# An attention block and a two-of-eight expert layer on one core: from 28 pair buckets to one list of slots per expert with the results added up in memory

## The chip, the core and the metric

The kernel runs on one core of one Trainium2 chip, in one launch. The metric is device time in microseconds: the median over the runs of the kernel, lower is better. Times inside a profile are microseconds from the start of the profiled span.

## What is computed

First a chunked attention over 4 batches, 8 heads, 768 tokens and 64 values per head: each chunk of 32 queries sees 8 memory keys of its batch and head and a window of 56 keys (16 to the left, its own 32, 8 to the right). Its output, with heads side by side, is a matrix x of 3072 tokens by 512. Then a noisy top-2 layer of 8 experts:

```python
noisy_logits = x @ w_gate + np.log1p(np.exp(x @ w_noise)) * noise
top2 = np.argpartition(-noisy_logits, 2, axis=1)[:, :2]
# top2_w: softmax over the two logits
for e in range(8):
    for k in range(2):
        mask = top2[:, k] == e
        h = np.maximum(x[mask] @ w1[e], 0.0)
        out[mask] += top2_w[mask, k, None] * (h @ w2[e])
```

`w1` is 512 by 1024 and `w2` is 1024 by 512 for each expert, all float32 in memory; the kernel computes in bfloat16. Every token goes to exactly two experts, so 6144 rows pass through an expert.

## The kernel before

**Attention.** The 32 heads of the 4 batches are worked on as 16 pairs (`NPAIR`), loaded in 8 groups of 2 pairs by `load_qk` (L109) and `load_v` (L118). These loads change float32 to bfloat16 on the way and are issued on GpSimd's queue (POOL). There are three buffers of each kind, so a load of group g waits until group g-3 is used up. A pair goes through TensorE transposes of q and k (L216, copied by ScalarE at L218), scores (L230 to L243), a maximum and a difference on VectorE (L251), an exponential on ScalarE, transposes of the probabilities, the product with v (`ps_o`, L279 and L282) and a division on VectorE into `xrow` (L294). The main loop over `i` (from L462 on) writes the order of every engine out by hand.

**Routing.** After 4 pairs a batch is complete. `route(b)` finds the two experts of each token, its gates and its rank within its bucket, and SyncE writes the batch's rows (`x_rows<-xrow`, 1056 bytes a token: 512 bfloat16 values and 8 gates) to memory.

**Experts.** A bucket holds the tokens that share the same pair of experts: 28 buckets with 128 slots each, and one spill tile of 32. Since a bucket belongs to two experts, its 128 rows are gathered once (`gather`, L580), transposed once into `xTb` (L589 copied at L590), and used by both. Expert e computes 7 buckets and the spill: `first` (L644) multiplies 928 columns by `w1`, relu alternates between ScalarE (L630) and VectorE (L632), `second` (L652) multiplies each of 7 tiles by `w2`. Of the two experts of a bucket the earlier leaves its scaled result in one of 20 accumulators on chip (ScalarE, L656); the later adds to it (VectorE, L659) and the row goes out by one scatter (L660). So `out` is written once and never read. Weights are loaded two experts ahead on POOL's queue by `load_w1` (L439) and `load_w2` (L444), three buffers each.

A loop for more than 32 spilled tokens stands at the end of the kernel; with the data used here it is not entered.

Of the kernel before, what the change touches and what calls it, by code (L numbers as in the profile page):

```python
# [14 lines left out]
F32R = mybir.dt.float32r  # L15
# [5 lines left out]
I32 = mybir.dt.int32  # L21
# [3 lines left out]
def kernel(  # L25
# [14 lines left out]
    nc = tc.nc  # L40
# [12 lines left out]
    HP = H // 2  # L53
    WIN = left_ctx + chunk + right_ctx
    CTX = WIN + n_mem
    SJ = S // 128
    assert D == 64 and CTX == 64 and 4 * chunk == 128 and S == 128 * SJ
    NPAIR = B * HP
    GP = 2
    NG = NPAIR // GP  # L60
    CAP = 128
    NB = E * (E - 1) // 2
    NB4 = E * (E // 2)
    SPILL = 32
    XC = Dm // 2
    ROW = XC + E
    FAR = 8 * N
    NEG = -1e30

    def bucket(a, b):  # L70
        d = b - a
        return (d - 1) * E + a if d <= E // 2 else (E - d - 1) * E + b

    xd = nc.dram_tensor("x_rows", [N, ROW], I32, kind="Internal").ap()
    xd_part = dram_disjoint_views(xd, B + 1)
    out_part = dram_disjoint_views(out, NB + 1)
# [4 lines left out]
    w1p = ctx.enter_context(tc.tile_pool(name="w1p", bufs=3))  # L81
    w2p = ctx.enter_context(tc.tile_pool(name="w2p", bufs=3))

    def body():
        actx = ExitStack()
        ap_ = actx.enter_context(tc.tile_pool(name="ap", bufs=2))
        psS = actx.enter_context(tc.psum_pool(name="psS", bufs=1))
        psO = actx.enter_context(tc.psum_pool(name="psO", bufs=1))
        psT = actx.enter_context(tc.psum_pool(name="psT", bufs=3))
        psL = actx.enter_context(tc.psum_pool(name="psL", bufs=1))  # L90

        nc.scalar.preload_act_table_set("natural_log_exp_and_others")


        groups = {}

        vbufs = [ap_.tile([128, GP, ncnk, 2, D], BF16, name=f"vg{i}", bufs=1) for i in range(3)]

        def new_group(g):
            qg = ap_.tile([128, 2 * GP, SJ * D], BF16, name="qg", bufs=3)  # L100
            kg = ap_.tile([128, 2 * GP, SJ * D], BF16, name="kg", bufs=3)
            groups[g] = (qg, kg, vbufs[g % 3])

        def load_qk(g, i=None):
            qg, kg, _ = groups[g]
            b, h0 = divmod(2 * GP * g, H)
            hs = slice(0, 2 * GP) if i is None else slice(2 * i, 2 * i + 2)
            for dst, src in ((qg, q), (kg, k)):
                nc.gpsimd.dma_start(out=dst[:, hs, :], in_=src[b, h0:h0 + 2 * GP][hs].rearrange("h (p j) d -> p h (j d)", p=128))  # L109
# [705 lines left out]
```

## Time and profile before

| | |
|---|---|
| median of 2 runs | 396.87 us (396.57 and 397.17) |
| span of the profiled execution | 393.1 us; 3.8 us of the median lie around it |
| PE (TensorE) busy | 304.5 us, 77% of the span |
| DVE (VectorE) busy | 169.9 us, 43% |
| ACT (ScalarE) busy | 119.8 us, 30% |
| POOL (GpSimd) busy | 124.5 us, 32% |
| moved by DMA | 42.93 MB in 83324 packets |

The profile gives busy times per engine, the same in stretches of the span ("windows", with the TensorE clock that was granted, the share of time in which the DMA engines worked, and the rate), the chain of work that ended last, groups of equal instructions with their mean duration, waits by what ended them, and a timeline. A share of DMA above 1 in a window means that packets of several transfers stood in the engines at once. PE, PEld, DVE, ACT and POOL are TensorE's products, its weight loads, VectorE, ScalarE and GpSimd; SP is SyncE, which only starts transfers here.

### The profile page before, as it was taken

The numbers are of one execution on the slowest core, as the hardware profiler recorded it, in microseconds if no ns is written. First come the engines' busy times: TensorE is split into PE (matmuls) and PEld (weight loads), VectorE is DVE, ScalarE is ACT, GpSimd is POOL, SyncE is SP. The second block draws the span as 40 slices with busy tenths as digits, with TensorE's granted clock in tenths as the row PEclk, the third lists the DMA queues.
The fourth block names the chain that finished last, engine by engine and source line by source line (L and its number), as shares of the span: only waits on it lengthen the run. The fifth ranks groups of instructions, "written<-read, shape, count | busy, mean of one in ns | idle before, by whom it ended". The sixth has DMA issues, their size and how long they took to land.

```text
span 393.1 us, 9217 instructions
## 1 busy us (share of the span) xinstructions
PE 304.5 (77%) x4042; PEld 188.6 (48%) x4060; DVE 169.9 (43%) x350; ACT 119.8 (30%) x235; POOL 124.5 (32%) x143
## 2 busy tenths in 40 slices
PE   0448688676846433888998998999998999999990
PEld 0436566454634322654465474454454454544540
DVE  7426345787757761342142242241433242443340
ACT  1436354565532200222333232233221312302200
POOL 7766234265000026352100420520605123032061
PEclk9999555898885655699999999999999999999997
DMA  9999999999970412849700291291492921811021
GB/s 92 100 164 156 158 152 94 167 150 141 211 154 3 143 46 80 151 82 216 141 0 2 45 221 30 64 209 34 97 213 88 191 56 71 132 67 70 3 115 59
DMA packets 83324, 42.93 MB, mean 109 GB/s; under 512 B 57255, under 2 KB 76711, under 8 KB 83280
## 3 DMA queue, kind: packets, MB, share of 16 engines
q0 software_dynamic: 74928, 38.85, 70.6%
q1 hardware_dynamic: 8064, 3.38, 3.4%
q8 instruction: 34, 0.56, 0.6%
q10 hardware_dynamic: 288, 0.07, 0.1%
q14 instruction: 10, 0.08, 0.1%
HBM read 61.32 MB, written 10.65 MB: 183 GB/s over the span
## 4 chain that ended last, share of the span: by engine, by line
PE 60%; DVE 15%; issue 10%; DMA 7%; ACT 3%; POOL 3%; POOLq 0%; DVEq 0%; ACTq 0%
PE ps_h L644 24%; PE ps_y L652 21%; DMA x_rows<-xrow 4%; PE p_t L216 3%; DMA kg<-in_k_dram 2%; PE ps_o L279 2%; PE ps_o L282 2%; DVE xrow L294 2%; PE p_t L589 2%; DVE vg L130 2%; DVE xTb L590 2%; POOL out_dram L660 2%; DVE mx L251 1%; ACT qT L218 1%; PE p_x L303 1%
## 5 line engine op out<-in xcount | busy, mean ns | idle before, releaser
L644 PE MATMUL ps_h<-xTb,w1t 128*128 128x512 bf16 (+3 forms) x608 | 107.8, 328 | 1.1 <-DVE xTb L590 1.0
L652 PE MATMUL ps_y<-w2t,ht 128*128 128x512 bf16 x430 | 98.9, 379 | 1.0 <-issue 0.2
L644 PEld LDWEIGHTS <-w1t 128*128 128x128 bf16 x864 | 64.7, 98 | 45.0 <-issue 1.1
L632 DVE TENSOR_SCALAR ht<-ps_h 128x416 bf16<-128x416 f32 (+2 forms) x68 | 41.7, 613 | 81.0 <-PE ps_h L644 81.0
L660 POOL DMA_INDIRECT out_dram<-acc,sidx x28 | 28.0, 998 | 144.9 <-DVE acc L659 142.4
L652 PEld LDWEIGHTS <-ht 128*128 128x128 bf16 x448 | 42.3, 98 | 48.9
L630 ACT ACTIVATE ht<-ps_h 128x416 bf16<-128x416 f32 (+2 forms) x68 | 36.3, 535 | 87.2 <-PE ps_h L644 83.1
L580 POOL DMA_INDIRECT xl<-x_rows,gidx x28 | 29.1, 1038 | 71.4 <-DVE ov1b L523 48.4
L644 PE MATMUL ps_h<-xTs,w1t 128*128 128x32 bf16 x256 | 45.4, 177 | 0.2 <-DVE xTs L605 0.2
L118 POOL DMA_DIRECT2D vg<-in_v_dram x34 | 32.9, 974 | 35.4 <-PE ps_o L282 29.8
L656 ACT ACTIVATE acc<-ps_y,meta 128x512 f32<-128x512 f32 x28 | 19.2, 687 | 76.5 <-PE ps_y L652 47.7
L659 DVE SCALAR_TENSOR_TENSOR acc<-ps_y,meta,acc 128x512 f32<-128x512 f32 x28 | 21.0, 751 | 38.6 <-PE ps_y L652 38.6
L590 DVE COPY xTb<-p_t 128x512 bf16<-128x512 bf16 x28 | 11.8, 423 | 27.1 <-PE p_t L589 26.9
L218 ACT CAST qT<-p_t 128x384 bf16<-128x384 f32 x32 | 16.9, 586 | 20.2 <-PE p_t L216 20.2
L216 PE MATMUL p_t<-identb,kg 128*64 128x128 bf16 x192 | 14.1, 275 | 10.5 <-ACT qT L218 7.7
L251 DVE TENSOR_REDUCE mx<-ps_s 128x12 f32<-128x768 f32 x16 | 15.2, 950 | 12.1 <-PE ps_s L243 12.1
L305 ACT COPY xt<-p_x 128x768 bf16<-128x768 bf16 x16 | 12.8, 799 | 22.5 <-PE p_x L303 22.5
L216 PE MATMUL p_t<-identb,qg 128*64 128x128 bf16 x192 | 11.5, 265 | 9.5 <-DMA qg<-in_q_dram 5.1
L279 PE MATMUL ps_o<-memv,PT 128*128 128x132 bf16 x96 | 11.2, 273 | 9.4 <-DVE PT L270 9.4
L589 PE MATMUL p_t<-identb,xl 128*128 128x128 bf16 x112 | 11.2, 224 | 8.9 <-DVE xTb L590 8.9
L218 ACT CAST kT<-p_t 128x384 bf16<-128x384 f32 x32 | 17.0, 597 | 2.0 <-PE p_t L216 1.7
L294 DVE TENSOR_TENSOR xrow<-ps_o,rec 128x768 bf16<-128x768 f32 x16 | 15.3, 958 | 5.3 <-DMA x_rows<-xrow 4.8
(128 smaller groups left out, 295.5 us busy)
## 6 DMA issues: line engine op xcount, KB each, us to landing
w1t<-in_moe_w_dram POOLq DMA_DIRECT2D x8, 1024.0 KB
w2t<-in_moe_w_dram POOLq DMA_DIRECT2D x8, 1024.0 KB
vg<-in_v_dram POOLq DMA_DIRECT2D x30, 168.0 KB
x_rows<-xrow SPq DMA_DIRECT2D x3, 792.0 KB, 6.3
qg<-in_q_dram POOLq DMA_DIRECT2D x6, 384.0 KB
kg<-in_k_dram POOLq DMA_DIRECT2D x6, 384.0 KB
qg<-in_q_dram POOLq DMA_DIRECT2D x4, 192.0 KB
kg<-in_k_dram POOLq DMA_DIRECT2D x4, 192.0 KB
```

The lines of the kernel that those rows point to most:

```text
L118: nc.gpsimd.dma_start(out=vg[p0 + j:p0 + j + nj, x, c:c + n, hh, :], in_=bass.AP(v.tensor, v.offset + (hd * S + c * chunk + j - left_ctx) ...
L216: nc.tensor.matmul(out=p_t[64 * hh:64 * hh + 64, j, :], lhsT=src[:, 2 * i + hh, (SH * x + j) * D:(SH * x + j + 1) * D], rhs=identb, start= ...
L218: nc.scalar.copy(dst[:, :, SH * x:SH * (x + 1)], p_t.rearrange("d j p -> d p j"))
L294: nc.vector.tensor_tensor(out=xr, in0=po.rearrange("p x (u h) c -> p x u h c", h=2)[:, :, :, :, :D], in1=rec.rearrange("p x (u h o) -> p x ...
L580: nc.gpsimd.indirect_dma_start(out=xl, out_offset=None, in_=xd, in_offset=bass.IndirectOffsetOnAxis(ap=gidx[:, p:p + 1], axis=0), bounds_c ...
L590: nc.vector.tensor_copy(xTv[:, :, p, :], p_t)
L630: nc.scalar.activation(out=dst, in_=src, func=Act.Relu)
L632: nc.vector.tensor_scalar(out=dst, in0=src, scalar1=0.0, scalar2=None, op0=Alu.max)
L644: nc.tensor.matmul(out=ps_h[:, o:o + w], lhsT=w1t[:, kp, f * 128:(f + 1) * 128], rhs=rhs(kp), start=(kp == 0 and i == 0), stop=(kp == KP - ...
L652: nc.tensor.matmul(out=ps_y, lhsT=ht[:, f, j * CAP:(j + 1) * CAP], rhs=w2t[:, f, :], start=(f == 0), stop=(f == FB - 1))
L659: nc.vector.scalar_tensor_tensor(out=a, in0=ps_y, scalar=gate, in1=a, op0=Alu.mult, op1=Alu.add)
L660: nc.gpsimd.indirect_dma_start(out=out_part[p], out_offset=bass.IndirectOffsetOnAxis(ap=sidx[:, p:p + 1], axis=0), in_=a, in_offset=None, ...
```

## The change

Everything in the kernel is written anew, around four decisions.

**A list scheduler sets the order.** Each step is an operation with candidate engines, an assumed duration, dependences, buffers and a priority. `Planner.run` simulates them and returns the operations in order of their simulated start; this is the order in which they are issued. Its costs are assumptions in the code: 1.05 for an indirect transfer plus 0.25 to 0.35 and 1.8 to 1.9 until it has landed, 3.0 and 3.4 for the two weight loads, 1.4 for a load of q or k, 3.1 for half a load of v.

**One list of slots per expert.** `x_lists` in memory has 3136 rows of 1060 bytes (values, gates, token number) for each expert. A batch writes each token's row to both of its lists: 12 indirect scatters per batch on POOL (L641), 48 in all, in place of one direct write by SP. The slots of an expert then lie side by side, so SP loads them with direct transfers (L684, L687) and the 28 gathers of rows are gone. Each expert computes 832 slots: a part of 512 and a tail of 320, whose last 64 rows are spread over two half rows each. All counts are below 832 for this data (715 to 808), so the loop at the end is not entered.

**Two experts are closed early.** Experts 0 and 1 take 512 slots from the first three batches alone ("sealed"), so their first parts need nothing from the last batch. Parts run in this order: sealed 0, sealed 1, experts 2 to 7 (512 and 320), tails of 0 and 1.

**Results are added up in memory.** `out` is filled with zeros by four SP transfers of 1.5 MB, and unused slots of the lists are blanked by one of 1.1 MB. Each tile of results is gathered from `out` (L751), added on VectorE (L776) and scattered back (L787); only sealed 0 scatters without gathering. That makes 52 gathers and 56 scatters in place of 29 scatters. A gather waits for all scatters of the experts before it, since two experts can share a token. In the expert stage relus are on ScalarE and additions on VectorE; 8 PSUM banks of one kind serve transposes, first and second products.

The attention keeps its steps. q and k are loaded as 96 partitions of 8 tokens, v in halves of 2 heads; the weights of experts 0 and 1 use buffers of their own and are loaded during attention.

```diff
-    CAP = 128
-    NB = E * (E - 1) // 2
-    SPILL = 32
+    CAPE = 3136
+    SEAL = 512
+    NSEAL = 2
+    CAP = 832
...
+    xs = nc.dram_tensor("x_lists", [E * CAPE, ROW], I32, kind="Internal").ap()
+    xs_part = dram_disjoint_views(xs, 2 * NP)
...
+    def run(self):
...
+                for eng, dur in o.engs:
+                    est = max(free.get(eng, 0.0), at)
+                    for d in o.deps:
+                        est = max(est, d.end if d.eng == eng and not d.dma else d.done)
+                    if best is None or est + dur < best[0] + best[2]:
+                        best = (est, eng, dur)
+                cand.setdefault(best[1], []).append((best[0], best[2], o))
...
+            for eng, cs in cand.items():
+                m = min(c[0] for c in cs)
+                c = min((c for c in cs if c[0] <= m + 0.25), key=lambda c: (c[2].prio, c[0]))
+                if pick is None or c[0] < pick[0]:
+                    pick = (c[0], c[1], c[2], eng)
...
+                xfer, lat = o.dma
+                dma_free = max(o.end + 0.6, dma_free) + xfer
+                o.done = dma_free + lat
...
+        return sorted(order, key=lambda o: o.start)
...
+        def qk_load(o, bb, src, b=b, h0=h0):
+            G_.dma_start(out=bb.t, in_=src[b, h0:h0 + 4].rearrange("h (p j) d -> p h (j d)", p=QP))
...
+            piece(int(first), 2 * ncnk - first - last)
+
+        zd = z_v[g] if g < 3 else []
+        lv = [op(("POOL", 1.3 if 0 < g < NG - 1 else 2.0), lambda o, hh=hh, f=v_load: f(o, hh), deps=zd, alloc=[bv] if hh == 0 else [], use=[] if hh == 0 else [bv],
+                 prio=pr + 6 + hh if g else 2 + hh, dma=(3.1, 1.6), tag="attn") for hh in range(2)]
...
+    c_fill = op(("SP", 0.1), lambda o: nc.sync.dma_start(
+        out=xs.rearrange("(e c) r -> c e r", c=CAPE)[CAP - 128:CAP], in_=blank.rearrange("p (o r) -> p o r", o=1).to_broadcast([128, E, ROW])),
+        deps=[z_bl, groups[1][4]], prio=20, dma=(3.0, 1.8))
...
+    c_zero = [op(("SP", 0.1), lambda o, i=i: nc.sync.dma_start(
+        out=out[i * S:(i + 1) * S].rearrange("(t p) d -> p t d", p=128), in_=zero.rearrange("p (o d) -> p o d", o=1).to_broadcast([128, BT, Dm])),
+        deps=[z_zero] + groups[NG - 1][5], prio=10.0 * NPAIR + i, dma=(2.8, 1.8)) for i in range(B)]
...
+                    G_.indirect_dma_start(
+                        out=xs_part[(b * BT + t) * 2 + kk], out_offset=bass.IndirectOffsetOnAxis(ap=R["idx"][:, t, kk:kk + 1], axis=0),
+                        in_=xr.t[:, t, :], in_offset=None, bounds_check=E * CAPE - 1, oob_is_err=True)
...
+                scat[b].append(op(("POOL", 1.05), scatter, deps=[r7, c_fill], use=[xr], prio=pr + 1 + 0.1 * t, dma=(0.25, 1.8)))
...
+    parts = []
+    for e in range(NSEAL):
+        parts.append(dict(e=e, s0=0, sealed=True, grp=e))
+    for x, e in enumerate(list(range(NSEAL, E)) + list(range(NSEAL))):
+        if e >= NSEAL:
+            parts.append(dict(e=e, s0=0, sealed=False, grp=NSEAL + x))
+        parts.append(dict(e=e, s0=SEAL, sealed=False, grp=NSEAL + x))
+    W = {}
...
+    def w_load(e, prio):
+        b1, b2 = buf("w1"), buf("w2")
+        o1 = op(("POOL", 0.85), lambda o: G_.dma_start(out=b1.t, in_=moe_w1[e].rearrange("(kp p) f -> p kp f", p=128)), alloc=[b1], prio=prio, dma=(3.0, 1.8))
+        o2 = op(("POOL", 0.95), lambda o: G_.dma_start(out=b2.t, in_=moe_w2[e].rearrange("(fb p) d -> p fb d", p=128)), alloc=[b2], prio=prio + 1, dma=(3.4, 1.8))
+        W[e] = (b1, b2, o1, o2)
+
+    for e in range(E):
+        w_load(e, 10.0 * 13.5 + e if e < NSEAL else 10.0 * NPAIR + 100 * e)
...
+            nc.sync.dma_start(out=bxl.t[:, :nf, :], in_=xs[r0:r0 + nf * 128].rearrange("(j p) r -> p j r", p=128))
+            if not full:
+                for hh in range(2):
+                    nc.sync.dma_start(out=bxl.t[64 * hh:64 * hh + 64, 2, :], in_=xs[r0 + 256:r0 + 320])
...
+        prev = [s for gnum in range(grp) for s in scatters.get(gnum, [])] + c_zero
...
+            def gather(o, b, R=R, t=t, w=w, oview=oview, bound=bound):
+                G_.indirect_dma_start(
+                    out=b.t[:, :w], out_offset=None, in_=oview(out), in_offset=bass.IndirectOffsetOnAxis(ap=R["ids"][:, t:t + 1], axis=0),
+                    bounds_check=bound, oob_is_err=False)
+
+            ga = None
+            if not plain:
+                ga = op(("POOL", 1.05), lambda o, f=gather, ba=ba: f(o, ba), deps=[oi] + prev, alloc=[ba], prio=pr + 6 + 0.1 * t, dma=(0.35, 1.9))
+            gy = buf("G", quota)
...
+                if plain:
+                    A.activation(out=ba.t[:, :w], in_=gy.t[:, :w], func=Act.Copy, scale=gate)
+                else:
+                    V.scalar_tensor_tensor(out=ba.t[:, :w], in0=gy.t[:, :w], scalar=gate, in1=ba.t[:, :w], op0=Alu.mult, op1=Alu.add)
+            yo = op(("ACT", 0.7) if plain else ("DVE", 0.25 + w / 960), yev, deps=[so, ga, lx] + (z_acc if plain else []), alloc=[ba] if plain else [], use=[gy, bxl] + ([] if plain else [ba]), prio=pr + 20 + t)
+            if plain and grp:
+                bb = buf("acc")
+                ga = op(("POOL", 1.05), lambda o, f=gather, bb=bb: f(o, bb), deps=[oi] + prev, alloc=[bb], prio=pr + 40 + 0.1 * t, dma=(0.35, 1.9))
+                yo = op(("DVE", 0.6), lambda o, ba=ba, bb=bb: V.tensor_tensor(out=ba.t, in0=ba.t, in1=bb.t, op=Alu.add), deps=[yo, ga], use=[ba, bb], prio=pr + 41)
...
+            def oscat(o, ba=ba, R=R, t=t, w=w, nv=nv, oview=oview, bound=bound):
+                G_.indirect_dma_start(
+                    out=oview(out_part[nv]), out_offset=bass.IndirectOffsetOnAxis(ap=R["ids"][:, t:t + 1], axis=0),
+                    in_=ba.t[:, :w], in_offset=None, bounds_check=bound, oob_is_err=False)
+
+            scatters.setdefault(grp, []).append(op(("POOL", 1.05), oscat, deps=[yo, oi] + c_zero, use=[ba], prio=pr + 20 + t, dma=(0.35, 1.8)))
```

Three places of the new order. The first is POOL's queue early in the attention, where the loads of group 3 begin (`qn` and `kn` are q and k, `vg` is v, `w1t` and `w2t` are the weights of experts 0 and 1):

```order
L376 DMA kn_103<-in_k_dram 96x4x512 [waits DMASW4_49,PE_49]
L659 DMA w1t_67<-in_moe_w_dram 128x4x1024 [waits DMASW5_49]
L376 DMA qn_101<-in_q_dram 96x4x512 [waits DMASW6_49,PE_49]
L660 DMA w2t_69<-in_moe_w_dram 128x8x512 [waits DMASW7_49]
L376 DMA kn_104<-in_k_dram 96x4x512 [waits DMASW0_49,PE_49]
L659 DMA w1t_68<-in_moe_w_dram 128x4x1024 [waits DMASW1_49]
L660 DMA w2t_70<-in_moe_w_dram 128x8x512 [waits DMASW2_49]
L387 DMA vg_105<-in_v_dram 56x48x64 [waits DMASW3_49,PE_49]
L387 DMA vg_105<-in_v_dram 56x48x64 [waits DMASW4_49]
```

All four weight loads of 1 MB now stand ahead of the two v loads of group 3; before, three weight loads stood behind the last v load of the whole attention:

```order
L118 DMA vg_89<-in_v_dram 48x64 [waits DMASW6_49]
L118 DMA vg_89<-in_v_dram 56x23x64 [waits DMASW7_49]
L439 DMA w1t<-in_moe_w_dram 128x4x1024 [waits DMASW0_49]
L444 DMA w2t<-in_moe_w_dram 128x8x512 [waits DMASW1_49]
L439 DMA w1t<-in_moe_w_dram 128x4x1024 [waits DMASW2_49]
L580 DMA xl<-x_rows,gidx 128x264 [waits DMAHW1_49,DMAHW2_49,DMAHW0_49,DMAHW3_49,DMASW3_49,DMAHW7_49,DVE_49,Activation_49]
```

The second place is POOL at the end of attention, between the scatters of the third batch (`xrow_87`) and of the last (`xrow_85`), with the weights of experts 2 and 3 between them (`w1l`, `w2l`):

```order
L641 DMA x_lists<-xrow_87,idx 25088x265 [waits DMASW5_49]
L659 DMA w1l_2976<-in_moe_w_dram 128x4x1024 [waits DMASW6_49,PE_49]
L660 DMA w2l_2978<-in_moe_w_dram 128x8x512 [waits DMASW7_49,PE_49]
L659 DMA w1l_2977<-in_moe_w_dram 128x4x1024 [waits DMASW0_49]
L660 DMA w2l_2979<-in_moe_w_dram 128x8x512 [waits DMASW1_49]
L641 DMA x_lists<-xrow_85,idx 25088x265 [waits DMAHW4_49,DMAHW5_49,DMASW2_49,DVE_49]
L641 DMA x_lists<-xrow_85,idx 25088x265 [waits DMASW3_49]
L641 DMA x_lists<-xrow_85,idx 25088x265 [waits DMASW4_49]
L641 DMA x_lists<-xrow_85,idx 25088x265 [waits DMASW5_49]
L641 DMA x_lists<-xrow_85,idx 25088x265 [waits DMASW6_49]
```

Rows further on wait for the transfers eight places ahead, so the fifth to eighth scatter of the last batch wait for the four weight loads to have landed. On PE, the first tile of expert 2 (`xll0`, loaded from the lists after all scatters) stands ahead of the products of sealed 1 (`w1t1`):

```order
L717 LDWEIGHTS xl1_72
L717 MATMUL ps_l3_3003<-identb_130,xl1_72 128x128
L717 LDWEIGHTS xll0_2980 [waits DMAHW6_49]
L717 MATMUL ps_l4_3004<-identb_130,xll0_2980 128x128 [waits DVE_49]
L717 LDWEIGHTS xll0_2980
L717 MATMUL ps_l4_3004<-identb_130,xll0_2980 128x128
L731 LDWEIGHTS w1t1_68 [waits DVE_49]
L731 MATMUL ps_l5_3005<-xT1_74,w1t1_68 128x512 [waits Activation_49]
```

What was behind the whole of sealed 1 in the list of parts is thus ahead of its first product in TensorE's order.

The third place is POOL during expert 3, from its last first-part gather to the first gather of expert 4 (L751 gathers from `out`, L787 scatters to it):

```order
L787 DMA out_0_dram<-acc4_81,ids_3281 3072x512 [waits DMASW4_49,DMASW5_49,DMASW3_49,DMASW6_49,DMASW2_49,DVE_49]
L787 DMA out_0_dram<-acc7_84,ids_3281 3072x512 [waits DMASW0_49,DVE_49]
L787 DMA out_0_dram<-accl1_2989,ids_3281 3072x512 [waits DVE_49]
L751 DMA accl0_2988<-out_0_dram,ids_3410 128x512 [waits DMASW7_49,DMASW1_49,DMASW0_49]
L787 DMA out_0_dram<-accl3_2991,ids_3281 3072x512 [waits DMASW2_49,DVE_49]
L751 DMA accl2_2990<-out_0_dram,ids_3410 128x256 [waits DMASW3_49]
L659 DMA w1l1_2977<-in_moe_w1_dram 128x4x1024 [waits PE_49]
L787 DMA out_0_dram<-acc6_83,ids_3410 3072x512 [waits DMASW4_49,DVE_49]
L787 DMA out_0_dram<-accl0_2988,ids_3410 3072x512 [waits DVE_49]
L660 DMA w2l1_2979<-in_moe_w2_dram 128x8x512 [waits PE_49]
L787 DMA out_0_dram<-accl2_2990,ids_3410 6144x256 [waits DVE_49]
L751 DMA accl4_2992<-out_0_dram,ids_3578 128x512 [waits DMASW7_49,DMASW6_49,DMASW1_49]
```

Before, the same place held scatters that no gather waited for, and gathers of rows that were there since attention:

```order
L439 DMA w1t<-in_moe_w_dram 128x4x1024 [waits DMASW7_49,PE_49]
L660 DMA out_dram<-acc_3309,sidx 3072x512 [waits DMASW0_49,DVE_49]
L660 DMA out_dram<-acc_3304,sidx 3072x512 [waits DMASW1_49,DVE_49]
L660 DMA out_dram<-acc_3298,sidx 3072x512 [waits DMASW2_49,DVE_49]
L444 DMA w2t<-in_moe_w_dram 128x8x512 [waits DMASW3_49,PE_49]
L580 DMA xl<-x_rows,gidx 128x264 [waits DMASW4_49,Activation_49]
L580 DMA xl<-x_rows,gidx 128x264 [waits DMASW5_49,Activation_49]
L439 DMA w1t<-in_moe_w_dram 128x4x1024 [waits DMASW6_49,PE_49]
```

Now gathers and scatters alternate, each waiting for the other to have landed, with the weight loads of expert 5 among them.

1175 lines of the change are left out of this document (561 added, 614 removed).

## The prediction

> **What bounds the kernel now.** I read the windows first, cut where the work changes, then the chain that ended last. In the windows the columns are length, busy time of PE, PEld, DVE, ACT and POOL, granted TensorE clock, DMA share and GB/s.
>
> ```profile
> 43.00:63.00 20.00, 15.73 (x394) 12.65 (x394) 10.22 (x15) 9.24 (x18) 7.49 (x8) 0.50 1.92 153
> 115.00:131.00 16.00, 9.28 (x203) 7.64 (x203) 12.62 (x29) 3.53 (x5) 0.00 (x0) 0.57 0.14 42
> 195.00:383.00 188.00, 183.57 (x1400) 97.68 (x1412) 64.86 (x106) 47.68 (x93) 46.16 (x47) 1.00 0.42 90
> 383.00:393.10 10.10, 0.11 (x1) 0.00 (x0) 0.75 (x1) 0.00 (x0) 1.41 (x2) 0.77 0.15 58
> ```
>
> There are two kernels in one. From 195 on PE works 183.57 of 188 us at full clock, seven experts of 26.9 us each, with DMA at 0.42: bound by PE. Before that no engine is full, and the transfers are another matter:
>
> ```profile
> DMA  9999999999970412849700291291492921811021
> POOL vg L118 <- PE ps_o L282: 29.8, 9, 5.3
> L294 DVE TENSOR_TENSOR xrow<-ps_o,rec x16: 957/958/958, 32.3 to 131.7; 128x768 bf16<-128x768 f32 x16
> 65.00:70.00 5.00, 0.96 (x1) 0.74 0.81 52
> 15.98 9.09 DMA kg<-in_k_dram
> 100.86 14.07 DMA x_rows<-xrow
> 128.25 3.34 DMA x_rows<-xrow
> ```
>
> The first row is the DMA engines' share in 40 slices of 9.8 us: at least 0.9 for the first 108 us. Yet POOL had room: its v loads waited 29.8 us for buffers that PE still used, so loads were ahead of compute. The third row is the division that ends each head pair, 16 times from 32.3 to 131.7; the seventh pair's falls in the window of the fourth row (that operation alone, one execution), at about 67. The last three are pieces of the chain: start, length, what. A 384 KB load took 9.09 us because others stood ahead in its queue, and 14.07 and 3.34 us were spent on the x rows, whose write shared the engines with weights. So this stage has no slack in transfers worth speaking of, and 17.4 us of pure waiting.
>
> **The change, part by part.** *What it saves.* PE's rows in an expert:
>
> ```profile
> 244.75 6.91 PE ps_y L652 x32
> 251.66 12.90 PE ps_h L644 x96
> L589 PE MATMUL p_t<-identb,xl 128*128 128x128 bf16 x112 | 11.2, 224 | 8.9 <-DVE xTb L590 8.9
> ```
>
> The first products take 12.90 us for 928 columns, so 11.6 for 832; four tiles of second products take 6.91, so the 6.5 tiles of an expert 11.2, with the half-row tail about 11.5; seven tiles of transposes are 28 of 224 ns in groups of four that overlap, some 1.6. PE needs 24.7 us an expert, in place of 26.9. If PE stayed the bound, eight experts would need 198 us. The 17.4 us on x rows fall away too.
>
> *Transfers ahead of group 3's v.* POOL's order puts four weight loads ahead of these v loads, and SP's four zero fills wait only for a memset, so they run at once. Prices, from windows in which one kind ran (weights, weights, q and k, v, output rows):
>
> ```profile
> 282.50:288.50 6.00, 6.00 (x48) 3.30 (x46) 2.33 (x4) 2.23 (x4) 2.45 (x3) 1.00 1.08 159
> 289.50:294.50 5.00, 4.95 (x37) 2.66 (x36) 1.93 (x3) 1.07 (x4) 0.05 (x1) 1.00 1.09 210
> 30.00:31.00 1.00, 1.00 (x13) 0.81 (x11) 0.00 (x0) 0.88 (x2) 0.36 (x1) 1.00 1.32 201
> 53.50:55.50 2.00, 1.19 (x22) 1.17 (x24) 0.76 (x2) 0.21 (x2) 1.42 (x2) 0.50 2.14 128
> 384.00:387.50 3.50, 0.00 (x0) 0.00 (x0) 0.00 (x0) 0.00 (x0) 0.98 (x1) 1.00 0.41 156
> ```
>
> 1 MB of weights at 159 to 210 GB/s is 5.0 to 6.6 us; I take 6.25 (four: 25). 384 KB of q or k at 201 is 2.0 (twelve: 24). Half a group of v is 344 KB, at 128 GB/s 2.6 (eight: 21). For rows of 2 KB written, 156 GB/s at a share of 0.41 is 380 at a full one: the 7.4 MB of zeros and blanks take 19 us, or 47 if they only get the 156; 19, because the row is the same kind of packet. With some 4 us until the first load the sum is 4 + 24 + 21 + 25 + 19 = 93 us for group 3's v. The seventh pair needs it at about 67 now, so it is 26 to 28 us late. The lower bound is no delay at all, if the fills and weights fit into gaps; against it speaks the row of nines. The nine later pairs took 131.7 - 67 - 17.4 = 47 us, so attention ends at about 142, and with the last ranking at 145.
>
> *The last batch's lists.* Prices of indirect transfers, in timelines of POOL and ACT:
>
> ```profile
> 143.89 1.16 POOL L580 DMA_INDIRECT xl<-x_rows,gidx  x1 [48.42 <-DVE ov1b L523]
> 145.35 1.04 POOL L580 DMA_INDIRECT xl<-x_rows,gidx  x1 [0.30 <-issue]
> 146.70 1.01 POOL L580 DMA_INDIRECT xl<-x_rows,gidx  x1 [0.30 <-issue]
> 147.04 0.20 ACT L591 COPY meta<-xl 128x8 f32<-128x8 f32 x1 [7.82 <-DMA xl<-x_rows,gidx]
> 384.17 0.98 POOL L660 DMA_INDIRECT out_dram<-acc,sidx  x1 [0.74 <-DVEq L738]
> 280.70 0.99 POOL L444 DMA_DIRECT2D w2t<-in_moe_w_dram  x1
> 284.41 0.85 POOL L439 DMA_DIRECT2D w1t<-in_moe_w_dram  x1
> ```
>
> One is issued every 1.3 us, and 3.1 us after its issue (143.89 to 147.04) another engine uses what came. I count 2.6 us to landing and 0.3 to the next issue. A scatter's is bounded by 384.17 and the 3.3 us to the end of its window, so the same value serves. The third batch's 12 scatters, queued behind the second's, run until 152.5; four weight loads are issued until 156 and move data until 179 or so; the fifth to eighth scatter of the last batch wait for these to land, and with four more behind them the last one lands at 188. The load of expert 2's first tile adds 3, an estimate from the same rows: X = 191. Since PE has that tile's transposes ahead of sealed 1's first product, sealed 1 cannot fill this gap; sealed 0 alone is done inside it. Now the first product of the expert stage starts at about 156 (chain: 157.69), so the early part costs 30 to 35 us.
>
> *An expert, by POOL's order.* Time from its first gather: five gathers 4 x 1.3 + 2.6 = 7.8; three scatters at 8.1, 9.4 and 10.7, landed at 13.3; a gather at 13.6, landed 16.2; a scatter at 16.5, landed 19.1; a gather at 19.4, landed 22.0; w1 issued at 20.7; two scatters at 22.3 and 23.6; w2 at 24.9; the last scatter at 25.9, behind 12.5 us of weights in the same queue, so landed at about 35.9. The next expert's first gather follows at 36.2. The additions in between cost little beside it:
>
> ```profile
> L659 DVE SCALAR_TENSOR_TENSOR acc<-ps_y,meta,acc 128x512 f32<-128x512 f32 x28 | 21.0, 751 | 38.6 <-PE ps_y L652 38.6
> ```
>
> 36.2 is more than PE's 24.7, so the chain of landings is the new bound. Its bounds: 24.7, if it all hides behind PE, and 36.2 + 0.75 for each of six alternations, 41. Expert 2 has its weights and needs 33.
>
> *The sum.* From X to expert 2's first gather 25 us (sealed 1's products, scatters and gathers); expert 2 33; experts 3, 4 and 5 36.2 each; so expert 6 begins at X + 166.6. It loads no weights: 28.5. Expert 7, seven gathers and then seven scatters, 9.1 + 2.6 + 0.3 + 9.1 + 2 = 22.5 or so. The first tail 12.3; the second 6.5 and its scatters, with the 8.9 us from the last scatter's issue (384.17) to the end of the span (393.1): 15.4. Together 78.7, so the span is 191 + 166.6 + 78.7 = 436, and with the 3.8 around it **440 us**; the profiled execution was 396.9 by the same addition, the same as the median of the runs.
>
> *The clock.* At 43 to 63 PE was busy for 79% and got a clock of 0.50; at 115 to 131, busy for 58%, 0.57. In the new expert stage it is busy for 68%, so it may not get a full clock there. At half, an expert takes PE 49.4 us in place of 24.7, and PE is the bound again. [...]
>
> **The rivals.**
>
> *A, PE stays the bound (faster).* Evict and gather overlap through eight PSUM banks and fourteen accumulators, early transfers fit into gaps. Then attention ends at 131.7 - 14 = 118, lists follow after four weight issues, twelve scatters and the load (3.6 + 15.6 + 2.6 + 3.3), at X = 143 to 147; after X PE needs 198 less the 15 of sealed 0, so 182, and 24 to the end with its last scatters: span 353, time **357**. It decides if gathers of an expert need not wait for the scatters just before. For it: POOL is busy only 46 of 188 us now. Against it: the order has the gathers wait for landings.
>
> *B, only the chain.* Fills and loads hide; attention ends at 119, 26 earlier than forecast, X = 165, the rest as forecast: 165 + 245 = 410, **414**. For it: the 29.8 us for which POOL waited. Against: the DMA row.
>
> *C, only the early part.* X = 191, but experts at PE's pace: 191 + 182 + 24 = 397, **401**. For it: gathers could be issued long before PE needs them. Against: only one expert's landings lie between two experts.
>
> *D, half clock in the expert stage.* Five experts at 49.4 in place of 36.2: 66 more, **506**. For it: the two rows of clock. Against: 1.00 wherever PE multiplied 512 columns at a stretch.
>
> **Chances.** Forecast 0.47, A 0.15, B 0.19, C 0.14, D 0.05. The forecast's own range, from an early part 8 shorter and the expert at 33 to one at 41, is 422 to 466. Leaving out A and D, 2 in 10, the range is 390 to 470, C's early end and the forecast's late one. A measurement tells about 2% from no change, 389 to 405: faster is A, 0.15; within 2% is most of C, 0.12; slower is the rest, 0.73.
>
> **What would show it.** In the new profile: PE idle before the seventh pair's `ps_o`, released by a v load, with the DMA row at nines to 90 us or beyond; the first `x_lists` tile of expert 2 transposed at about 190; in the expert stage a period of 36 us, PE busy for about 70% of it, VectorE's additions at L776 waiting for gathers from `out`, and POOL's gathers waiting for scatters. The forecast is wrong if PE is busy over 90% there (A or C), if the seventh pair ends before 75 us (A or B), or if the clock there is near 0.5 (D).

## The result, and the profile after

The changed kernel takes **505.84 us** (503.51 to 508.17) where the kernel before takes 396.87: slower by a factor of 1.276, 95% interval 1.261 to 1.290. Slower was forecast, with 440 us and a range to 470; the forecast missed 66 us. The profiled span is 506.5 us, against a forecast of 436.

Two rows of the profile's page, in slices of 12.7 us: the share of the DMA engines, and the granted clock.

```profile
DMA  9999999997920399364357745852963774243220
PEclk9999997675656555989987995995798698589985
```

The transfers are dense (0.7 or more in every slice) to 139 us, where they were to 118 before. What follows is new: a long end of attention with little DMA from 139 to 177, and an expert stage that alternates between work and none. In windows cut where that changes (the columns are those of the prediction):

```profile
13.00:36.00 23.00, 18.34 (x469) 15.30 (x466) 12.92 (x19) 10.65 (x14) 1.50 (x3) 1.00 1.25 301
36.00:58.00 22.00, 2.40 (x42) 1.92 (x36) 0.85 (x8) 1.11 (x2) 7.32 (x18) 1.00 2.29 187
58.00:98.00 40.00, 28.42 (x701) 23.73 (x700) 22.76 (x51) 17.83 (x25) 15.06 (x16) 0.84 1.76 184
98.00:188.00 90.00, 54.64 (x1100) 42.08 (x1089) 38.76 (x94) 22.52 (x34) 46.65 (x47) 0.58 1.16 120
285.77:413.23 127.46, 79.80 (x462) 41.31 (x470) 22.50 (x57) 29.80 (x57) 48.12 (x48) 0.83 0.62 144
```

From 36 to 58 us almost nothing computes (PE 2.40 us of 22). From 98 to 188 PE is busy for 61%, at a clock of 0.58, and attention ends there. The last row is experts 3, 4 and 5, first gather to first gather: 127.46 us, 42.5 each, in which PE works 79.80, or 26.6 each. Before, PE worked 183.57 of 188 us.

**The first stop.** The second half of the third group's v is issued 20 us late. One row each of SP, POOL and VectorE, and the first and seventh divisions:

```profile
13.35 14.08 SPq L528 DMA_DIRECT2D out_dram<-zero  x4
35.92 1.38 POOL L387 DMA_DIRECT2D vg<-in_v_dram  x1 [20.36 <-issue]
57.02 0.17 DVE L323 CAST eb<-eb_i 128x8 f32<-128x8 int32 x1 [24.12 <-POOL eb_i L315]
62.80 0.22 DVE L486 RECIPROCAL rec<-ps_o 128x12 f32<-128x12 f32 x1
98.31 0.23 DVE L486 RECIPROCAL rec<-ps_o 128x12 f32<-128x12 f32 x1 [6.22 <-PE ps_o L481]
```

While the four zero fills go out, 301 GB/s move in the first window: 5.77 of its 6.91 MB are on the queue that carries SP's zeros and blanks. POOL stands 20.36 us at a v load; POOL's own constants (`eb_i`) are further down its queue; VectorE, in its order, has the copy of `eb_i` ahead of the next scores, and stops for 24.12 us. The first division of a head pair comes at 62.80, where the kernel before had its one at 32.3.

**The second.** In the window of 98 to 188 lie the slow scores: PE's score products, 0.8 to 0.9 us a pair in ten of the sixteen pairs and 1.94 in one, last 2.70, 4.88, 4.62, 8.44 and 6.99 us in the other five. Rows of PE's weight loads in one of these, and of POOL at the same time:

```profile
141.78 0.13 PEld L448 LDWEIGHTS <-qT 64*32 64x32 bf16 x3 [0.61 <-issue]
142.51 0.14 PEld L448 LDWEIGHTS <-qT 64*32 64x32 bf16 x4 [0.60 <-issue]
143.96 0.15 PEld L448 LDWEIGHTS <-qT 64*32 64x32 bf16 x4 [1.31 <-issue]
...
140.80 0.98 POOL L641 DMA_INDIRECT x_lists<-xrow,idx  x1 [0.30 <-issue]
142.09 0.98 POOL L641 DMA_INDIRECT x_lists<-xrow,idx  x1 [0.30 <-issue]
```

PE waits for nothing the profile names ("issue"), and gets through three or four loads and then stands for 0.60 to 1.31 us, a halting pace, though such a group lasts only 0.13 to 0.15. All five slow pairs lie where POOL issues scatters into the lists, and in this run no other pair does.

**The third** is an expert. POOL's rows of expert 3, then VectorE's and PE's where they meet them:

```profile
291.10 1.01 POOL L751 DMA_INDIRECT acc<-out_dram,ids  x1 [0.30 <-issue]
295.79 1.02 POOL L787 DMA_INDIRECT out_dram<-acc,ids  x1 [3.68 <-DMA acc<-out_dram,ids]
298.41 0.98 POOL L787 DMA_INDIRECT out_dram<-accl,ids  x1 [0.30 <-issue]
301.94 1.05 POOL L751 DMA_INDIRECT accl<-out_dram,ids  x1 [2.55 <-DMA out_dram<-accl,ids]
306.06 1.01 POOL L787 DMA_INDIRECT out_dram<-accl,ids  x1 [3.07 <-DMA accl<-out_dram,ids]
310.01 1.03 POOL L751 DMA_INDIRECT accl<-out_dram,ids  x1 [2.95 <-DMA out_dram<-accl,ids]
...
312.28 0.48 DVE L776 SCALAR_TENSOR_TENSOR accl<-ps_l,xl,accl 128x256 f32<-128x256 f32 x1 [6.13 <-DMA accl<-out_dram,ids]
312.68 0.41 DVE L288 COPY xT<-ps_g 128x512 bf16<-128x512 bf16 x1
313.24 0.59 PE L731 MATMUL ps_l<-xT,w1l 128*128 128x512 bf16 x1 [12.83 <-DVE xT L288]
323.04 1.89 PE L764 MATMUL ps_l<-w2l,ht 128*128 128x512 bf16 x8
327.45 1.06 POOL L751 DMA_INDIRECT accl<-out_dram,ids  x1 [9.91 <-DMA out_dram<-accl,ids]
330.95 0.75 DVE L776 SCALAR_TENSOR_TENSOR accl<-ps_l,xll,accl 128x512 f32<-128x512 f32 x1 [9.68 <-DMA accl<-out_dram,ids]
```

Gather, add, scatter, gather, 4 us at each landing, as forecast in kind. But behind the last addition of an expert (312.28) VectorE has the copies of the next expert's transposed rows (312.68), and only then does PE's first product start, after 12.83 us idle. The first addition of the next expert comes at 330.95, 18.7 us later, and its last at 356.11, 25.2 us after that. Two chains run side by side through the 18.7 us. PE's products start behind the copies and fill 17.43 of the 17.75 us from 313.20 on; the first tile of second products (323.04) is done at 324.9. POOL's last scatter, issued at 316.53, lands behind two weight loads, and the next expert's first gather waits 9.91 us for it, until 327.45. The addition at 330.95 waits for that gather, not for PE: the chain that ended last in experts 3 to 5 runs through landings, additions and POOL. PE's chain is nearly as long.

### The profile page after: what moved, and what is told of

Read it like the earlier page. It is cut to its first block, busy times and chain, and to the rows that moved or that the text cites. A ratio compares the mean times of both kernels' runs of the same rounds, so it can differ in the third digit from the quotient of the medians.

```text
span 506.5 us, 8737 instructions
## 1 busy us (share of the span) xinstructions
PE 322.3 (64%) x3573; PEld 198.9 (39%) x3596; DVE 150.6 (30%) x361; ACT 139.3 (28%) x238; POOL 210.3 (42%) x225
## 4 chain that ended last, share of the span: by engine, by line
DMA 22%; issue 14%; PE 9%; POOL 5%; DVE 2%; POOLq 1%; DVEq 0%; SPq 0%
DMA acc<-out_dram,ids 7%; DMA out_dram<-acc,ids 6%; DMA out_dram<-accl,ids 5%; PE ps_l L731 4%; PE ps_l L764 3%; POOL out_dram L787 3%; DMA accl<-out_dram,ids 3%; PE ps_g L731 2%; POOL accl L751 2%; POOL acc L751 1%; DVE acc L776 1%; DMA xll<-x_lists 1%; DVE accl L776 1%; PE ps_g L764 0%; DVE xTl L288 0%
## 5 line engine op out<-in xcount | busy, mean ns | idle before, releaser
L731 PEld LDWEIGHTS <-w1l 128*128 128x128 bf16 x384 | 39.9, 105 | 105.4 <-issue 80.7
L641 POOL DMA_INDIRECT x_lists<-xrow,idx x48 | 47.8, 995 | 55.5 <-DVE ids_f L700 18.0
L731 PE MATMUL ps_l<-xTl,w1l 128*128 128x320 bf16 (+1 forms) x193 | 41.4, 363 | 36.3 <-DVE xTl L288 33.7
L751 POOL DMA_INDIRECT acc<-out_dram,ids x30 | 30.8, 1028 | 53.4 <-DMA out_dram<-acc,ids 44.8
L787 POOL DMA_INDIRECT out_dram<-acc,ids x34 | 34.0, 1000 | 45.4 <-DVE acc L776 10.0
L737 ACT ACTIVATE htl<-ps_l 128x320 bf16<-128x320 f32 (+1 forms) x55 | 27.8, 507 | 70.8 <-PE ps_l L731 61.0
L751 POOL DMA_INDIRECT accl<-out_dram,ids x22 | 22.6, 1029 | 40.0 <-DMA out_dram<-accl,ids 35.8
L737 ACT ACTIVATE ht<-ps_l 128x512 bf16<-128x512 f32 (+1 forms) x40 | 21.2, 533 | 45.8 <-PE ps_l L731 35.1
L787 POOL DMA_INDIRECT out_dram<-accl,ids x22 | 21.9, 998 | 27.1 <-issue 8.3
L764 PE MATMUL ps_l<-w2l,htl 128*128 128x512 bf16 x138 | 32.1, 379 | 0.3
L764 PEld LDWEIGHTS <-ht 128*128 128x128 bf16 x176 | 17.5, 100 | 21.4 <-issue 3.4
L418 PE MATMUL ps_q<-identb,kn 96*64 96x96 bf16 x256 | 22.5, 411 | 0.5 <-ACT qT L286 0.4
```

Of the source, the lines that this page charges most:

```text
L418: P_.matmul(out=d[64 * hh:64 * hh + 64, t // 4, t % 4, :], lhsT=s[:, j + 2 * hh, t, :], rhs=identb[:QP, :QP], start=True, stop=True)
L641: G_.indirect_dma_start(out=xs_part[(b * BT + t) * 2 + kk], out_offset=bass.IndirectOffsetOnAxis(ap=R["idx"][:, t, kk:kk + 1], axis=0), in ...
L731: P_.matmul(out=gh.t[:, :n], lhsT=b1.t[:, kp, f * 128:(f + 1) * 128], rhs=bxT.t[:, kp, :n], start=(kp == 0), stop=(kp == KP - 1))
L737: A.activation(out=bht.t[:, f, :n], in_=gh.t[:, :n], func=Act.Relu)
L751: G_.indirect_dma_start(out=b.t[:, :w], out_offset=None, in_=oview(out), in_offset=bass.IndirectOffsetOnAxis(ap=R["ids"][:, t:t + 1], axis=0),
L764: P_.matmul(out=y, lhsT=bht.t[:, f, 128 * t:128 * (t + 1)], rhs=b2.t[:, f, :], start=(f == 0), stop=(f == FB - 1))
```

## The experiments

Each is an edit of the changed kernel. Runs of the kernel before on the chips used here gave 385 to 398 us, so runs of different chips are compared by their ratio or by times inside the profiles.

### fills_late

```diff
+    put([z_zero] + c_zero, behind=pairs[9]["ml"])
```

`put` takes operations out of the planned order and sets them in elsewhere.

> The four zero fills of out, and the memset that they wait for, come after the tenth head pair. Queue theory (the fills held POOL's loads back from 13 to 36 us, and everything behind them): VectorE's stop from 32.9 to 57.0 us shrinks to under 8 us, the first division is done before 40 us in place of 63, and the whole takes 480 to 496 us. Rival (the loads are late by their own bytes): that stop stays over 18 us and the time is 500 to 508. Clock theory (PE at half clock in the expert stage sets the end): no change beyond what attention gains; nothing in the experts' periods.

495.67 us, beside 397.61 for the kernel before (1.247). The window of 13 to 36, then VectorE's wait and the first division:

```profile
13.00:36.00 23.00, 18.10 (x420) 15.05 (x417) 12.44 (x18) 10.91 (x14) 6.59 (x9) 1.00 2.60 161
```

```profile
41.22 0.17 DVE L323 CAST eb<-eb_i 128x8 f32<-128x8 int32 x1 [8.60 <-POOL eb_i L315]
47.01 0.22 DVE L486 RECIPROCAL rec<-ps_o 128x12 f32<-128x12 f32 x1
```

The stop falls from 24.12 to 8.60 us and the first division comes 15.8 us earlier: the fills held POOL's loads. A stop under 8 us and a division before 40 were expected. Of these 15.8 us some 10 reach the end, as far as single runs on different chips can tell.

### iota_first

```diff
+    put([c_pool], behind=c_ident)
```

> Only the constants that POOL makes (iotas, masks) come ahead of its loads. If the queue behind the blocked loads is what stopped VectorE, its wait for eb_i (24.1 us) is gone. If memv's loads, which stand behind the same blocked loads, are late as well, PE's first product with v still waits until 55 to 62 us, and the total changes by 0 to 8 us: 498 to 506. If the constants alone were the cause, 480 to 485.

503.35 us (ratio 1.266). VectorE no longer waits for `eb_i`, and the first division comes at 58.52, released by PE's `ps_o`: what that product needs, v or the memory values, was late as well. The constants alone cost 4.3 us there, at most.

### weights_after_v

```diff
+    put([w for e in range(NSEAL) for w in W[e][2:]], behind=max((o for g in groups for o in g[5]), key=order.index))
```

> Only the four weight loads of experts 0 and 1 go behind the last v load of attention. The step of the prediction that put them ahead of group 3's v at 6.25 us each: the seventh pair's division, now at 98.3 us, comes 15 to 25 us earlier, and what of it reaches the end is 8 to 20 us (486 to 498), since scatters into the lists still slow PE behind it. Rival (v was late for the fills alone): the seventh pair stays at 94 to 99 us and the total within 3 us of 506.

492.69 us beside 385.32 (1.279). The seventh pair's division comes at 92.75 in place of 98.31. The four loads ahead of group 3's v cost it 5.6 us here, where the fills still come first, not 25; that lies between the two expectations. (`no_gather`, on the same chip and with attention as it is in the changed kernel, has this division at 97.35.) The last division comes at 145.60 in place of 183.93, but most of that is not this edit's: `no_gather` has it at 150.97.

### early_all

The three edits together.

> Fills behind the tenth head pair, POOL's constants first, weights of experts 0 and 1 behind the last v load. If the three early causes add, the first division is at 38 to 45 us and the seventh pair's before 75 us, and the whole takes 465 to 485 us. If PE is slowed by the issue of the scatters that follow in any case, the last division still comes after 150 us and the whole takes 485 to 497.

490.38 us beside 385.32 (1.273). The first division is at 46.18, the seventh at 77.64, a little over what was expected, and the last at 129.85, 54 us earlier than in the changed kernel (183.93). Yet the last batch's first scatter starts only 14 us earlier, and the total's ratio is as it was. POOL's rows show where the rest went:

```profile
122.73 0.98 POOL L641 DMA_INDIRECT x_lists<-xrow,idx  x1 [10.18 <-DMA vg<-in_v_dram]
127.70 0.98 POOL L641 DMA_INDIRECT x_lists<-xrow,idx  x1 [3.99 <-DMA w1t<-in_moe_w_dram]
132.75 0.98 POOL L641 DMA_INDIRECT x_lists<-xrow,idx  x1 [4.06 <-DMA w2t<-in_moe_w_dram]
182.61 1.06 POOL L641 DMA_INDIRECT x_lists<-xrow,idx  x1 [14.85 <-issue]
```

Against `no_gather` (150.97, and 178.22 for that scatter) attention ends 21 us earlier and the scatter comes 4 us later. The scatters of the second batch wait for weight loads in their queue, those of the third are issued behind them, one every 1.29 us until 163.4, then four weight loads; the last batch's wait until the lists of the sealed experts have been read (the second is there at 181.01). With attention early, POOL's queue sets the start of the experts:

| | last batch's first scatter | first gather of expert 2 |
|---|---|---|
| changed kernel | 196.84 | 248.54 |
| fills_late | 180.4 | 235.6 |
| weights_after_v | 180.8 | 235.8 |
| early_all | 182.6 | 236.7 |

### lists_direct

The scatters into the lists become direct transfers of the same rows, which therefore go to the wrong lists.

```diff
-                    G_.indirect_dma_start(
-                        out=xs_part[(b * BT + t) * 2 + kk], out_offset=bass.IndirectOffsetOnAxis(ap=R["idx"][:, t, kk:kk + 1], axis=0),
+                    G_.dma_start(out=xs_part[n][r0:r0 + 128], in_=xr.t[:, t, :])
```

> The 48 scatters into the lists become direct transfers of the same rows from the same queue, to places in order (rows go to the wrong lists). Issue theory (while POOL issues indirect transfers, PE's small instructions come in fours every 0.7 us): the scores of every pair take 0.9 us again in place of 2.7 to 8.4 in five pairs, attention ends 15 to 30 us earlier, 475 to 490 in all. Rival 1 (traffic of the rows, or the half clock, slows PE): the same pairs still take over 2.5 us, and the time is over 495.

472.62 us beside 397.61 (1.189), better than expected. Scores take 0.81 to 0.89 us in all pairs but one (2.71) from the third on. A pair while POOL issues rows:

```profile
138.40 0.32 PE L439 MATMUL ps_s<-mkT,qT 64*128 64x8 bf16 x12
138.71 0.55 PE L448 MATMUL ps_s<-kT,qT 64*32 64x56 bf16 x40
...
138.55 2.14 POOL L643 DMA_DIRECT2D x_lists<-xrow  x4 [1.13 <-DMA x_lists<-xrow]
```

Bytes and rows are the same and the clock is hardly better (0.66 from 98 to 152, 0.59 in the changed kernel), so neither traffic nor clock slowed the scores; once the indirect form is taken away, the halting pace is gone. (The 2.71 us hold one stop of 1.68.) But the indirect form does not do it alone: `no_gather`, below, issues the same indirect scatters, one every 1.29 us, and its scores beside them take 0.81 to 0.96 us. Of the runs with indirect scatters, those on the chips of `early_all` and `order_rounds`, five in all, show at most one stop in a set of scores beside scatters; those on the other chips all show the halting pace. The changed kernel itself was not run on these two chips, so what has to come together with the scatters, the chip or something else, is open. Direct transfers also take POOL half a microsecond each (2.14 us for the four in the last row), where an indirect scatter takes 1.29, so the run does not divide the gain of some 30 us (first scatter into `out` at 184.3 in place of 215.42) between PE and POOL's queue.

### together

```diff
+        put(sorted(ga, key=order.index)[1:], behind=first)
+        put(ws, behind=max(sc, key=order.index))
```

For each of experts 2 to 7: seven gathers, seven scatters, then weights.

> In experts 2 to 7 POOL issues the seven gathers together, then the seven scatters, then the weights. Chain theory (six landings in turn of 3.5 to 4.1 us, and 11 us behind weights): experts 3 to 5 go from 42 to 44 us down to 32 to 36, expert 6 from 34 to about 25, the whole 450 to 470. Clock theory (half clock sets the period): the periods stay over 40 us and the time within 2% of 506.

446.02 us beside 397.61 (1.122). Experts 3 and 4 take 27.9 us each. The window from expert 3 to the end of expert 5, then POOL's first gather and first scatter of expert 3:

```profile
269.80:355.00 85.20, 72.88 (x449) 38.77 (x447) 22.23 (x57) 28.93 (x58) 47.60 (x48) 0.96 0.86 215
```

```profile
269.76 1.08 POOL L752 DMA_INDIRECT acc<-out_dram,ids  x1 [0.87 <-DMA out_dram<-acc,ids]
286.56 1.02 POOL L790 DMA_INDIRECT out_dram<-acc,ids  x1 [7.81 <-DVE inv L699]
```

An expert beats the least that was expected by 4 us, and PE is busy for 86%: with all gathers issued ahead, no addition stands behind a landing that waits for the scatter before it.

### weights_last

```diff
+        if ws:
+            put(ws, behind=max(sc, key=order.index))
```

Only the weights are moved; gathers and scatters still alternate.

> Only the two weight loads of each expert are moved, behind its last scatter; gathers and scatters still alternate. It divides the 14 us an expert that the order of seven and seven saved. If the loads in the queue cost 8 to 10 of them, the experts come to 32 to 35 us; if the alternation costs most, they stay at 37 to 42.

493.01 us beside a median of 394.5 (1.250; the unchanged kernel, below, 1.277 on that chip). Experts 3 to 5 begin 40.0, 41.8 and 38.4 us apart, by POOL's rows, against 41.1, 43.9 and 41.5 there. So the alternation costs most of what `together` gains, the place of the loads 2 or 3 us. The next expert's gathers now stand behind the loads instead, and PE's products run in that time; the chain that ended last goes through them, from 307.63 to 327.55:

```profile
306.67 0.48 DVE L779 SCALAR_TENSOR_TENSOR accl<-ps_l,xl,accl 128x256 f32<-128x256 f32 x1 [6.07 <-DMA accl<-out_dram,ids]
326.02 0.75 DVE L779 SCALAR_TENSOR_TENSOR accl<-ps_l,xll,accl 128x512 f32<-128x512 f32 x1 [14.60 <-DMA accl<-out_dram,ids]
```

From an expert's last addition to the next one's first it is 19.4 us, where the changed kernel has 18.7.

### no_gather

The gathers from `out` are left out, and each expert scatters into a tensor of its own, so results are not added up.

```diff
-                    out=oview(out_part[nv]),
+                    out=oview(out_part[nv] if grp == 0 else y_part[grp][nv]),
```

> The 52 gathers from out are left out and every expert scatters its results into a tensor of its own, not added up. Chain theory: experts run at PE's pace, 25 to 28 us each in place of 37 to 44, and the whole takes 415 to 440 us. Clock theory (PE at half clock): the periods stay over 36 us, the whole over 470.

396.18 us beside 385.32 (1.028). In the expert stage:

```profile
216.00:340.00 124.00, 123.17 (x758) 66.55 (x771) 40.59 (x97) 50.94 (x97) 43.04 (x45) 1.00 0.73 172
```

PE works 123.17 of these 124.00 us, and the granted clock is 1.00; weight loads come 24.4 to 26.0 us apart. The clock theory is out: without the gathers this stage ran at full clock. `weights_after_v`, on the same chip and with attention ending as early, takes 492.69, so the gathers and what waits for them cost some 96 us. Even without them this run is not faster than the kernel before.

The attention of this run is that of the changed kernel, and it issues its scatters at the same pace, yet the scores do not halt:

```profile
142.74 0.98 POOL L642 DMA_INDIRECT x_lists<-xrow,idx  x1 [0.30 <-issue]
144.03 0.98 POOL L642 DMA_INDIRECT x_lists<-xrow,idx  x1 [0.31 <-issue]
...
143.16 0.32 PE L440 MATMUL ps_s<-mkT,qT 64*128 64x8 bf16 x12 [0.15 <-DVE sd L457]
143.47 0.55 PE L449 MATMUL ps_s<-kT,qT 64*32 64x56 bf16 x40
```

### lists_first

```diff
+    put([z_zero] + c_zero, behind=pairs[15]["ml"])
+    put([w for e in (2, 3) for w in W[e][2:]], behind=max(scat[3], key=order.index))
-            idx = R["idx"] = T("idx", [128, BT, 2], I32)
+            idx = R["idx"] = rt.tile([128, BT, 2], I32, name="idx", bufs=4)
```

with the edits of iota_first, weights_after_v and together.

> The best order so far: POOL's constants first, weights of experts 0 and 1 behind the last v load, those of 2 and 3 behind the last batch's scatters, fills behind the last pair, four index buffers, experts in the order of seven gathers, seven scatters, weights. If POOL's own queue (48 scatters of 1.29 us and the landings eight places ahead) now sets the start of the experts, the first gather of expert 2 comes at 200 to 215 us in place of 236, and the ratio to the kernel before is 1.02 to 1.07. If the start hangs on something else, it stays over 230 us and the ratio at 1.10 to 1.13.

459.32 us (median of four; ratio 1.161, interval 1.145 to 1.178): slower than both expectations, and than `together`. The first gather of expert 2 is at 258.1, later than in the changed kernel. Two rows say why:

```profile
157.91 0.96 DVE L455 TENSOR_REDUCE mx<-ps_s 128x12 f32<-128x768 f32 x1 [20.71 <-remote]
237.37 1.07 POOL L752 DMA_INDIRECT acc<-out_dram,ids  x1 [24.67 <-DMA out_dram<-acc,ids]
```

Beside seventeen scatters in one stream (133.6 to 154.2) the last pair's scores took at least 12.9 us; and the four weight loads, now ahead of the sealed experts' scatters, kept these 24.67 us from landing.

### after_again

The changed kernel unedited, on the chip of the two before it.

> The changed kernel once more, unchanged, beside the next ones on one chip. If the stages do not depend on the chip, expert 3 to 6 begin 41 to 44 us apart and the ratio to the kernel before is 1.26 to 1.30.

503.77 us beside 394.5 (1.277); the last batch's first scatter is at 194.6, experts 3 to 5 begin 41.1, 43.9 and 41.5 us apart.

### both_out

no_gather and lists_direct in one, with the early edits of fills and constants; rows go to wrong lists and results are not added up.

> Three causes taken out at once: direct transfers in place of the scatters into the lists (rows go to the wrong lists), no gathers from out (results of each expert to a tensor of its own, not added up), and the early order (POOL's constants first, fills behind the tenth pair). If these are all that kept the change from PE's pace, the time comes near the prediction's rival A: 340 to 365 us. If something else holds it too, 370 to 395.

370.45 us beside a median of 387.47 (0.956): the lower end of the second expectation, something else holds it too.

```profile
175.00:345.00 170.00, 168.59 (x1057) 91.80 (x1075) 53.55 (x133) 72.62 (x138) 59.05 (x63) 1.00 0.65 162
```

From 175 on PE is the bound again, as in rival A. What keeps it from rival A's 357 lies before 175, where a v load is 12 us late once more and the lists come late; that was not taken apart further.

### order_rounds

early_all's edits and together's, in rounds.

> The early order together with seven gathers, seven scatters, weights, now timed in rounds. Single runs gave 432 and, for the order alone, 446, each 1.12 of the kernel before on its chip. If the early order is worth 10 us or more at the end, the ratio is 1.08 to 1.11; if POOL's scatters take it back whole, 1.11 to 1.14. Either way slower than before.

430.04 us (median of five) beside 387.47: 1.110, interval 1.102 to 1.117, the best version that computes the whole result, still slower than before. Its first gather of expert 2 is at 236.0, together's at 245.7; the ratio lies on the border between the two expectations and does not decide. An earlier single run of the same edits (`early_together`), on the chip of `early_all`, took 432.15 us beside 385.32. It was expected at 415 to 436 if the gains of the two stages add, and at 436 to 444 if the early one is taken back. The time falls in the first range, but its ratio, 1.122, is that of `together`, so the early gain is not shown.

## Why the prediction was wrong

It named the sign and both mechanisms: early transfers that hold back group 3's v and the last lists, and experts bound by landings in memory. Its sum fell 70 us short of the span: 32.5 at the first gather of expert 2 (248.5, not 216), 28.7 over experts 2 to 6 (198.9 to the first gather of expert 7, not 170.1) and 8.9 from there to the end. Two steps failed: the pace of attention behind the seventh pair, and the size of a landing in an expert.

*"A gather at 13.6, landed 16.2 ... The next expert's first gather follows at 36.2."* The path was right, for the chain that ended last follows it; its links were too short. Experts 3 to 5 took 41.7, 44.1 and 41.7 us, over the stated bound of 41. From one issue to the next the prediction counts 2.9 us, 2.6 to landing and 0.3. In expert 3 a gather behind a scatter came after 3.53 and 3.95 us, and a scatter behind a gather, with the addition between them that the sum put at nothing, after 4.69 and 4.12. So from the fifth gather's issue to the last one's landing it is 21.2 us (291.10 to 312.28), not 16.8, and the last scatter is issued 30.8 us after the first gather, not 25.9. The wait behind the weights was sized well: 10.9 us, against 10.3. `together` removed the alternation and saved 14 us an expert. What the prediction did not see is the second chain: VectorE's copies stand behind the last addition, so PE's products are not free to run beside the alternation and fill the time of the last link. So `weights_last`, which moved the weight loads out of that link, saved only 2 or 3.

*"93 us for group 3's v", "26 to 28 us late".* The time of the seventh division, 98.3, came out close to the forecast, by another way. The fills did not fit in beside POOL's loads, they held them up and stopped the first pairs (in `fills_late` the stop of 24.12 us fell to 8.60); the weights in front of the v cost 5.6 us.

*"The nine later pairs took ... 47 us, so attention ends at about 142."* This failed by 42 us: the last division was at 183.93, and the nine pairs took 85.6. The pace of before was carried over to a stage in which POOL issues 36 scatters. The five stretched scores alone are 27.6 - 5 x 0.87 = 23.3 us. `lists_direct` shows that they go with the indirect form of the scatters, `no_gather` that this form does not stretch them by itself; the cause stays open, and the remaining 15 us were not divided. The last ranking was forecast at 3 us; the first scatter behind it came 12.9 us after the last division (196.84). The first `x_lists` tile of expert 2 was transposed at 218.14, where X was 191.

*"The fifth to eighth scatter of the last batch wait for these to land"* was right for the queue (`early_all` shows such waits of 4 us each, for the second batch) but not on the path here: with attention late, the weights had landed when the last batch was ready, and from 196.84 on its twelve scatters were issued 1.3 us apart. So 27 of the 42 us show in X.

*PE's price*, 24.7 us an expert, held: no_gather's loads come 24.4 to 26.0 us apart. *Rival A* failed for its condition, not its price: both_out brings its expert stage. *Rival D*, half clock, forecast 506 us, and the time came out at 505.84; that is chance. PE was idle for 37% of experts 3 to 5, and its clock there was 0.83. What the clock does cost can be read at a restart:

```profile
357.07 0.59 PE L731 MATMUL ps_l<-xTl,w1l 128*128 128x512 bf16 x1 [15.20 <-DVE xTl L288]
357.88 5.75 PE L731 MATMUL ps_l<-xTl,w1l 128*128 128x512 bf16 x18 [0.22 <-issue]
363.47 1.89 PE L731 MATMUL ps_g<-xTl,w1l 128*128 128x512 bf16 x8
```

After 15.2 us of idling the first 18 products take 5.75 / 18 = 0.32 us each, the next eight 1.89 / 8 = 0.24. The granted clock was 0.50 from 357.07 to 361, 0.85 from 361 to 362 and 1.00 from 362 to 365.36; by the two rates this restart costs about 18 x 0.08 = 1.5 us.

## What to carry to other kernels

A chain through memory is to be followed on every engine it crosses: the order of one queue gave its landings, but the engine that does the additions also did the copies that start the next stage, in order, and so PE's first product of the next expert came after 12.83 us of idling. Issue reads that depend on the same earlier writes together, and the dependent writes together; alternating them paid every landing here (41.7 to 44.1 us an expert, 27.9 in `together`), and a landing is to be counted to the next issue, with what lies between (3.53 to 4.69 us in expert 3, where 2.9 was forecast). And when a stage is made earlier, ask at once which queue takes over as its end: in `early_all` attention ended 54 us earlier and the last batch's scatters began 14 us earlier. Last, when an effect goes away with a part of the kernel, look for a run that kept that part and lacks the effect too: here `no_gather` was that run.

## What the runs showed of the hardware

In the changed kernel, while POOL issued indirect transfers, PE got through its small instructions a few at a time (three or four weight loads, then a halt of 0.60 to 1.31 us in the rows of the result; 2.70 to 8.44 us for a set of scores that otherwise takes 0.87), and the profile names nothing that it waited for. With direct transfers of the same rows that pace was gone (`lists_direct`); with indirect ones on another chip it did not appear either (`no_gather`, 0.81 to 0.96). What brings it on stays open. In expert 3 a gather that waited for a scatter was issued 3.53 and 3.95 us behind it, 128 rows each. Four fills of 1.5 MB from SyncE's queue moved, with the rest, at 301 GB/s, and a v load of POOL's was issued 20 us late; with the fills later the same stretch moved 161 GB/s and PE's first results came 15.8 us earlier. The kernel before took from 385 to 398 us on the chips of these runs.
